# Moving all late weights behind a transpose on one DMA-issuing engine, and choosing an instruction order by its mean in noisy replays

## The chip, the cores and the metric

The kernel runs on one core of one Trainium2 chip. The metric is the device time of one execution in microseconds (us), lower is better. A run over 1.5% above the fastest of its kernel counts as "slow" and is left out. The "granted clock" is the share of full speed at which PE was allowed to run.

Engines in the listings: PE is the matmul engine (PEld its weight load), DVE the vector engine, ACT the scalar engine, POOL the GpSimd engine, SP the engine that issues nearly all DMA here (SPq in a listing is its DMA issuing).

## The reference, cut to what matters

Two layers, each a linear-attention block A and a gated block B, applied twice with the same weights to a 2048 x 512 sequence:

```python
def reference(A_x, A_wqkv, A_w_phi, A_wo, B_x, B_W_gate, B_W_up, B_W_down):
    # A: q, k, v = x @ wqkv ; phi = softmax(+-(. @ w_phi)) ; kv = sum over the sequence of phi_k * v
    #    out = (phi_q @ kv) / (phi_q @ z) @ wo
    # B: (relu(x @ W_gate) * (x @ W_up)) @ W_down
    x = A_x
    x = x + _A_ref(_layernorm(x), A_wqkv, A_w_phi, A_wo)
    x = x + _B_ref(_layernorm(x), B_W_gate, B_W_up, B_W_down)
    x = x + _A_ref(_layernorm(x), A_wqkv, A_w_phi, A_wo)
    x = x + _B_ref(_layernorm(x), B_W_gate, B_W_up, B_W_down)
    return x
```

The sum over the whole sequence (kv) closes the first phase: no output of A can be made before all 16 tiles of 128 rows have gone through k, v and the normalisation of phi_k.

## The kernel before

The program lists operations with what they read and write, and a list scheduler with a model of durations picks an order for every engine. Each engine then runs its instructions strictly in that order. In the first phase a tile `t` passes through:

1. layer norm "apply" into one of four buffers (`ytile`), on DVE for even tiles, on ACT for most odd ones;
2. a DMA transpose into `yT`, issued by SP (tiles 4 to 15; tiles 0 to 3 use PE);
3. k and v projections on PE, exponentials and copies on ACT;
4. a sum (`Zk`) and reciprocal (`rZk`) on DVE, then the product `phik` on POOL (half of it on DVE for tiles 14, 15);
5. accumulation `kvacc` on PE. After tile 15, DVE evicts the sums to `kvbd`, and the next phase begins.

SP also issues the late weights: eight pieces of `wo` (64 KB each), four of `Wg`, four of `Wu` (344 KB each), six of `Wd`. They are needed only after the first phase. Before, they were sprinkled among the transposes, each waiting for a `phik`:

```python
        def kv(t, n):
            ...
            for tt in range(t, t + n):
                self.kv_acc(tt, "A0")
                for _ in range(1 if 4 <= tt < 12 else 2):
                    if pieces:
                        pieces.pop(0)(self.r("phik", tt, 0))
        L(1); kv(0, 1); kv(1, 1); L(2); kv(2, 1); kv(3, 1)      # (one call a line in the kernel)
        self.compose_q(); kv(4, 2); L(3); kv(6, 2); kv(8, 2); kv(10, 2)
        self.q_proj(0, qr0, "A0")
        kv(12, 2); kv(14, 1); kv(15, 1)
        self.kv_fin("A0")
```

The scheduler tries 48 orders and kept the one with the shortest span in its model. In that model a weight costs SP 450 ns to issue and a transpose 1190 ns.

The softmax here doesn't subtract the row's maximum and nothing guards it: scores larger than these inputs give would overflow.

## Time and profile before

| | before |
|---|---|
| time, median of 3 | 396.07 us (395.46 to 396.57) |
| PE busy | 381.1 of 394.1 us |
| PE idle from 9 to 65 us, then up to 242 us | about 4.6 us, then none |
| tile 12's transpose: issued, landed | 36.81, 41.03 us |
| first `kvbd` eviction | 54.26 us |
| first Wg matmul (block B begins) | 74.85 us |

The first part of the profile of before gives busy time, share of the span and number of instructions:

```profile
PE 381.1 (97%) x2320; PEld 207.1 (53%) x2320; DVE 274.3 (70%) x634; ACT 215.8 (55%) x421; POOL 110.1 (28%) x160
```

Busy time by stretch of the kernel before (start:end, length, then each engine's busy us and instruction count, granted clock, DMA share, GB/s) shows where PE is not busy:

```profile
20.00:30.00 10.00, 9.89 (x69) 5.28 (x67) 10.00 (x18) 10.00 (x15) 9.28 (x11) 1.00 0.47 84
30.00:40.00 10.00, 9.08 (x67) 5.04 (x68) 9.12 (x13) 6.72 (x8) 10.00 (x6) 1.00 0.64 150
40.00:50.00 10.00, 9.58 (x71) 5.15 (x70) 7.82 (x11) 7.71 (x13) 7.79 (x5) 1.00 0.85 225
50.00:56.00 6.00, 5.54 (x57) 3.53 (x55) 4.61 (x10) 2.81 (x6) 3.82 (x3) 1.00 0.75 239
56.00:65.00 9.00, 6.84 (x53) 3.68 (x51) 7.18 (x23) 8.62 (x17) 0.00 (x0) 1.00 0.14 29
```

PE is the limit nearly everywhere; a change of order can win back little more than the few idle microseconds from 9 to 65 us (from 242 to 252 us there are 1.1 more). POOL has no idle time from 30 to 40 us. The timeline of SP in the kernel before (start, length of the issuing, what, how many) shows weights between the transposes:

```profile
31.81 2.58 SPq L536 DMA_TRANSPOSE yT<-ytile  x2
34.43 1.23 SPq L502 DMA_DIRECT2D wo_p<-in_A_wo_dram  x2
35.71 1.06 SPq L505 DMA_DIRECT2D Wg<-in_B_W_gate_dram  x2
36.81 1.22 SPq L536 DMA_TRANSPOSE yT<-ytile  x1
38.08 1.07 SPq L505 DMA_DIRECT2D Wg<-in_B_W_gate_dram  x2
39.20 1.19 SPq L536 DMA_TRANSPOSE yT<-ytile  x1
```

The transpose at 36.81 is tile 12's, the one at 39.20 tile 14's. Tile 12's input was ready at about 33.5 us. The chain that ended last, in order of time, passes through it:

```profile
36.81 4.22 DMA yT<-ytile
41.04 0.05 issue
41.08 1.05 PE ps L587 x4
42.14 0.02 issue
42.16 1.95 ACT expk L590 x2
```

It takes 4.22 us to land (median of all: 2.4), and k of tile 12 starts on its landing. POOL's timeline shows what that does to the `phik` products, idle time and releaser in brackets:

```profile
41.68 3.81 POOL L573 TENSOR_TENSOR expk<-expk,rZk 128x1024 bf16<-128x1024 bf16 x2 [0.62 <-DVE rZk L570]
47.08 6.74 POOL L573 TENSOR_TENSOR expk<-expk,rZk 128x1024 bf16<-128x1024 bf16 x4 [1.59 <-ACT expk L559]
```

### The profile page before, as it was taken

What the parts mean: (1) busy time and instruction counts of PE and PEld (TensorE: products, weight loads), DVE (VectorE), ACT (ScalarE), POOL (GpSimd) and SP (SyncE); (2) the same over time, 40 slices, a digit from 0 to 9 for tenths busy, and PEclk for the clock granted to TensorE, in tenths of its full rate; (3) what the DMA queues carried; (4) which work ended last, traced back from release to release, by engine and by line L of the source; (5) the groups of instructions that cost most, each with busy time, mean ns of one, the idle gap of its engine ahead of it and who ended that gap; (6) DMA issues with size and microseconds to landing.
All of it is one profiled execution on the core that took longest, in us unless ns stands there. A gap on an engine that the chain in (4) does not pass through costs nothing.

```text
span 394.1 us, 6313 instructions
## 1 busy us (share of the span) xinstructions
PE 381.1 (97%) x2320; PEld 207.1 (53%) x2320; DVE 274.3 (70%) x634; ACT 215.8 (55%) x421; POOL 110.1 (28%) x160
## 2 busy tenths in 40 slices
PE   5998997999999999999999999899999999999996
PEld 3455463676744444444444457467774454444442
DVE  5999778886865888886765777997875576421332
ACT  5897769953744412633354475997573562453440
POOL 5399741211000122383344543121101011100000
PEclk9999999999999999999999999999999999999999
DMA  6845942221211222311100110232323122100001
GB/s 189 217 86 147 240 146 53 55 54 28 55 28 27 42 54 54 68 27 15 27 14 2 27 28 2 41 68 54 68 55 67 27 42 67 29 27 0 28 27 53
DMA packets 61518, 23.00 MB, mean 58 GB/s; under 512 B 53456, under 2 KB 60464, under 8 KB 61488
## 3 DMA queue, kind: packets, MB, share of 16 engines
q1 hardware_dynamic: 60912, 22.08, 24.7%
q10 hardware_dynamic: 576, 0.52, 0.5%
q8 instruction: 18, 0.29, 0.3%
q14 instruction: 12, 0.10, 0.1%
HBM read 7.91 MB, written 2.10 MB: 25 GB/s over the span
## 4 chain that ended last, share of the span: by engine, by line
PE 83%; DVE 7%; issue 3%; DMA 3%; ACT 2%; POOL 2%; SPq 0%; DVEq 0%; POOLq 0%
PE ps L696 39%; PE ps L720 19%; PE ps L556 7%; PE ps L675 7%; PE ps L629 5%; PE ps L645 3%; PE ps L602 2%; DVE stats L516 2%; POOL expk L573 2%; DVE rZk L570 1%; DMA yT<-ytile 1%; DVE Zk L568 1%; DMA x_sb<-in_A_x_dram 1%; ACT numbf L649 1%; DMA oT<-osb 1%
## 5 line engine op out<-in xcount | busy, mean ns | idle before, releaser
L696 PE MATMUL ps<-yT,Wu 128*128 128x512 bf16 (+3 forms) x440 | 128.2, 336 | 0.0
L696 PE MATMUL ps<-yT,Wg 128*128 128x512 bf16 (+3 forms) x440 | 128.0, 336 | 0.0
L698 ACT ACTIVATE gate_sb<-ps 128x512 bf16<-128x512 f32 (+3 forms) x110 | 55.8, 512 | 100.8 <-PE ps L696 86.1
L720 PE MATMUL ps<-Wd,hT 128*128 128x512 bf16 (+1 forms) x352 | 107.7, 379 | 0.0
L573 POOL TENSOR_TENSOR expk<-expk,rZk 128x1024 bf16<-128x1024 bf16 (+1 forms) x32 | 59.6, 1879 | 31.6 <-DVE rZk L570 16.2
L520 POOL TENSOR_SCALAR rv<-mv 128x1 f32<-128x1 f32 (+1 forms) x55 | 13.0, 238 | 190.1 <-DVE mv L517 187.7
L696 PEld LDWEIGHTS ps<-yT,Wu 128*128 128x128 bf16 (+1 forms) x440 | 43.8, 100 | 33.4 <-ACT expk L703 0.8
L696 PEld LDWEIGHTS ps<-yT,Wg 128*128 128x128 bf16 (+1 forms) x440 | 43.5, 100 | 33.4 <-ACT gate_sb L698 0.9
L649 ACT ACTIVATE numbf<-ps 128x432 bf16<-128x432 f32 (+1 forms) x96 | 44.1, 500 | 18.1 <-PE ps L645 16.9
L720 PEld LDWEIGHTS ps<-Wd,hT 128*128 128x128 bf16 (+1 forms) x352 | 34.1, 98 | 36.8 <-DVE x_sb L722 0.9
L705 DVE TENSOR_TENSOR hT<-gate_sb,expk 128x512 bf16<-128x512 bf16 (+3 forms) x73 | 25.9, 355 | 34.2 <-ACT expk L703 33.0
L516 DVE BATCH_NORM_STATS2 stats<-x_sb 128x6 f32<-128x512 bf16 x64 | 42.7, 683 | 4.8 <-DMA x_sb<-in_A_x_dram 4.5
L568 DVE TENSOR_REDUCE Zk<-expk 128x64 f32<-128x1024 bf16 x32 | 37.9, 1202 | 6.3 <-ACT expk L559 3.1
L675 PE MATMUL ps<-wo_p,oT 128*128 128x512 bf16 x128 | 39.9, 379 | 1.6 <-DMA oT<-osb 1.6
L722 DVE TENSOR_TENSOR x_sb<-x_sb,ps 128x512 bf16<-128x512 bf16 x32 | 21.7, 685 | 27.1 <-PE ps L720 27.0
L703 ACT ACTIVATE expk<-ps 128x512 bf16<-128x512 f32 (+3 forms) x73 | 36.1, 497 | 1.1 <-PE ps L696 1.0
L645 PE MATMUL ps<-kvbd,expq 128*128 128x144 bf16 x256 | 35.1, 226 | 0.9 <-ACT numbf L649 0.6
L629 PE MATMUL ps<-yT,Wqp 128*128 128x512 bf16 x128 | 34.7, 379 | 0.9 <-ACT expq L632 0.7
L521 POOL TENSOR_TENSOR rstd<-rv,mhalf 128x1 f32<-128x1 f32 (+1 forms) x55 | 34.0, 620 | 4.1
L632 ACT ACTIVATE expq<-ps 128x1024 bf16<-128x1024 f32 (+1 forms) x40 | 32.4, 858 | 4.2 <-PE ps L629 3.8
L708 DVE TENSOR_TENSOR hT<-gate_sb,ps 128x512 bf16<-128x512 bf16 (+2 forms) x37 | 22.6, 614 | 16.8 <-PE ps L696 14.4
L559 ACT ACTIVATE expk<-ps 128x512 bf16<-128x512 f32 x44 | 23.8, 596 | 19.2 <-PE ps L556 18.9
(57 smaller groups left out, 393.3 us busy)
## 6 DMA issues: line engine op xcount, KB each, us to landing
out_dram<-x_sb SPq DMA_DIRECT2D x16, 128.0 KB, 1.7
x_sb<-in_A_x_dram SPq DMA_DIRECT2D x3, 512.0 KB, 6.1
Wg<-in_B_W_gate_dram SPq DMA_DIRECT2D x4, 344.0 KB, 4.2
Wu<-in_B_W_up_dram SPq DMA_DIRECT2D x4, 344.0 KB, 4.5
Wd<-in_B_W_down_dram SPq DMA_DIRECT2D x5, 256.0 KB, 3.3
yT<-ytile SPq DMA_TRANSPOSE x60, 2.4
hT<-in_A_wqkv_dram ACTq DMA_DIRECT2D x4, 128.0 KB, 3.0
x_sb<-in_A_x_dram SPq DMA_DIRECT2D x4, 128.0 KB, 3.7
```

The source lines that it names most:

```text
L516: op("dve", (lambda t: lambda e: e.bn_stats(k.stats6[:, t, :], k.x_sb[:, t, :]))(t), [r("x", t)], [r("st", t)], 685, f"{tag} stats {t}")
L521: op("pool", lambda e: e.tensor_tensor(k.rstd[:, t0:t1, :], k.rv1[:, t0:t1, :], k.mhalf[:, 0:n], ALU.pow), [r("rv1", t) for t in ts] + [r( ...
L568: op("dve", lambda e: e.tensor_reduce(k.Zk[:, zb, :], k.expk[:, t, :, :].rearrange("p s (h f) -> p (s h) f", f=16), AX.X, ALU.add), [r("ex ...
L573: op(eng, (lambda s0, s1: lambda e: e.tensor_tensor(k.expk[:, t, s0:s1, :].rearrange("p s (h f) -> p (s h) f", f=16), k.expk[:, t, s0:s1, ...
L629: op("pe", (lambda c, ic, bank: lambda e: e.matmul(k.pb[bank][:], k.Wqp[:, ic, c * 128:(c + 1) * 128], k.yT[:, ic, st * 512:(st + 1) * 512 ...
L645: op("pe", (lambda s, c, j, g0, bank: lambda e: e.matmul(k.pb[bank][:, j * GW:(j + 1) * GW], k.expq[:, st, c, s, tt * 128:(tt + 1) * 128], ...
L649: op("act", (lambda g0, n, bank: lambda e: e.activation(k.numbf[:, b, g0:g0 + n, :], k.pb[bank][:, 0:n * GW].rearrange("p (g m) -> p g m", ...
L675: op("pe", (lambda c, bank: lambda e: e.matmul(k.pb[bank][:], k.oT[:, ob, c, :], k.wo_p[:, c, :], start=(c == 0), stop=(c == NC - 1)))(c, ...
L696: op("pe", (lambda bank, W, ic, fc, Mf: lambda e: e.matmul(k.pb[bank][0:Mf, 0:n], W[:, ic, fc * 128:fc * 128 + Mf], k.yT[:, ic, c0:c0 + n] ...
L698: op("act", (lambda Mf, gb, gs: lambda e: e.activation(k.gate_sb[0:Mf, gs, 0:n], k.pb[gb][0:Mf, 0:n], ACT.Relu))(Mf, gb, gs), [self.RP[gb] ...
L703: op("act", (lambda Mf, ub, tu: lambda e: e.activation(k.expk[0:Mf, tu, 0, 0:n], k.pb[ub][0:Mf, 0:n], ACT.Copy))(Mf, ub, tu), [self.RP[ub] ...
L720: op("pe", (lambda fc, Kf, u, c0: lambda e: e.matmul(k.pb[bank][:], k.hT[0:Kf, u, c0:c0 + 128], k.Wd[0:Kf, fc, :], start=(fc == 0), stop=( ...
```

## The change

Its intent: SP first issues all transposes of the first phase, then all late weights, in one block. And of the 48 candidate orders, the one with the lowest mean span over six replays with noisy durations is taken, to be robust against errors of the model.

```diff
+    TRIALS = 6
...
+        rng = random.Random(1)
+        noise = [[rng.uniform(0.92, 1.08) for _ in ops] for _ in range(self.TRIALS)]
...
-                span = max(finish)
+                span = self._replay(order, noise)
...
+    def _replay(self, order, noise):
+        ...   # run the fixed order with each duration times its noise, return the mean of the spans
...
             for tt in range(t, t + n):
                 self.kv_acc(tt, "A0")
-                for _ in range(1 if 4 <= tt < 12 else 2):
-                    if pieces:
-                        pieces.pop(0)(self.r("phik", tt, 0))
...
         L(3)
+        for i, piece in enumerate(pieces):
+            piece(self.r("yT", 15 if i < 8 else 15))
         kv(6, 2)
```

Each piece now depends on the transpose of tile 15. That tile has the highest number, but the scheduler is free to issue another tile's transpose after it. The order of SP in the built kernel, by operation names:

```
before: tr 4 5 6 7 | wo0 wo1 | tr 9 11 | wo2 wo3 | tr 8 | wo4 wo5 | tr 13 15 10 | wo6 wo7 Wg0 Wg1 | tr 12 | Wg2 Wg3 | tr 14 | Wu Wd
after:  tr 4 5 6 7 9 8 11 13 10 15 12 | wo0 ... wo7 | tr 14 | Wg0 Wu0 Wg2 Wu3 Wg1 Wu2 Wg3 Wu1 | Wd
```

More of the change, by code (lines that the diff above doesn't have):

```diff
@@ L1 @@
+import random
 from contextlib import ExitStack
@@ L141, in schedule @@
                 prio = [t - o.boost for t, o in zip(self._backward(start, finish), ops)]
-        self.makespan, start, finish, order = best
+        _, start, finish, order = best
+        self.makespan = max(finish)
         for o in ops:
@@ L201, in _forward @@
         return start, finish, order
+    def _replay(self, order, noise):
+        ops = self.ops
+        total = 0.0
+        for f in noise:
+            free = {e: 0.0 for e in ENG_NAMES}
+            fin = [0.0] * len(ops)
+            q_free = 0.0
+            for i in order:
+                o = ops[i]
+                t = free[o.eng]
+                for d in o.deps:
+                    t = max(t, fin[d] + (self.SAME_LAT if ops[d].eng == o.eng else self.SYNC_LAT))
+                free[o.eng] = t + o.dur * f[i]
+                if o.is_dma:
+                    q_free = max(t + self.DMA_FIXED * 0.35, q_free) + o.dma_bytes / self.DMA_BW * (3 * f[i] - 2)
+                    fin[i] = q_free + self.DMA_FIXED * 0.65 * (5 * f[i] - 4)
+                else:
+                    fin[i] = free[o.eng]
+            total += max(fin)
+        return total / len(noise)
     def _backward(self, start, finish):
```

## The prediction

The prediction was written before any run of the changed kernel. Its "order listing" is a comparison of the two built programs, instruction by instruction on each engine.

> **What bounds the kernel now.** TensorE: the profile's first part gives PE 381.1 us of a 394.1 us span, the chain of waits 83%. Sixteen 128x512 matmuls in that chain take 3.46 us, and both kernels issue 880,896 matmul columns, so the pure stream is an estimated 372 us. Of the 22 us lost, most lie in the first 9 us and from 9 to 65 us, about 3 after the last matmul. From 65 to 242 and from 252 to 383 us PE is never idle (busy time by stretch): nothing is to be had there.
>
> **What the change does.** Same instructions, same bytes; only orders move. By the order listing POOL moves one phik, ACT and DVE agree from the first GLU stretch on, SP moves the weights. Before, eight wo pieces (0.62 us of SP each) and four Wg pieces (0.53) stand between the twelve yT transposes (1.2 to 1.3 each). Tile 12's, ready at about 33.5 us, is issued at 36.81 and lands 4.22 us later (median 2.4); its k projection starts at 41.08, at that landing. That starves ACT, then DVE (2.19 us idle before Zk 12 at 44.1), then POOL: idle 0.62 us before 41.68 and 1.59 before 47.08. Otherwise POOL runs the phik products without a gap from 25.8 to 53.8 us, 1.91 us each, and the last ends the phase (the chain shows phik, kvacc, kvbd).
>
> **What that is worth.** After: eleven transposes, all wo (5.0 us), tile 14's transpose, Wg/Wu interleaved, Wd. Tile 12 lands at about 36 us, so k of 12 and 13 starts some 3 us sooner. Tile 14's transpose stays at 39 to 40 us, no longer slowed by Wg. POOL caps the gain: the gaps are 2.2 us, plus at most 0.3 to 0.5 from its earlier second product. I expect the first kvbd at 52.0 instead of 54.26 us.
>
> Given back: all of Wg, Wu, Wd (4.2 MB) is issued from about 40.5 us; at the 240 GB/s that the slices show that takes an estimated 17.5 us, to 58, where it was over at about 56. The first oT transposes, then due at 57, meet its end. (The Trainium skill, "DMA: Bandwidth & Descriptors", Queues, rings and completion order: descriptors are consumed in ring order; tile 12's 4.22 us agrees.) I take 0.3 us off. The next stretch, to 75 us, is held by ACT (8.6 of 9, then 9.5 of 10 us busy) and only shifts. The noise-averaged choice changes no work and, where PE is saturated, nothing that counts: 0 ± 0.5 us.
>
> **Prediction: 394.0 us**, 8 in 10 between 392.4 and 395.6. Faster by over 2%: 0.02, within 2%: 0.97, slower by over 2%: 0.01.
>
> **What would show each step.** Right: the SP queue has its yT transposes back to back and the eleventh by 35 us; POOL idles under 0.6 us from 26 us to its last phik, which ends at 51 to 52; the first Wg matmul (74.85) starts near 72.9; from then on the traces run 2 us apart to the end. Wrong: POOL still idles before tiles 12 to 15; the first oT transpose takes over 3.5 us or is issued behind Wd; PE waits on Wg, Wu or Wd.
>
> **What would make it wrong.** Tile 14 behind eight wo pieces lands after 43 us and becomes the new wait; weights collide with oT transposes more than I think; the new order of q and wo matmuls between 56 and 75 us stalls ACT or DVE; or the shift is absorbed later, from 242 to 252 us or in the tail.

## The result, and the profile after

The changed kernel took 395.77 us (median of 4, 395.43 to 395.92), the kernel before 395.94 (4 runs). The ratio was 0.9994, 95% interval 0.9976 to 1.0011. A ratio is the mean time of one kernel's fast runs over that of the other's in the same rounds, so it is not quite the ratio of the medians. The prediction's 394.0 us (392.4 to 395.6) was missed. A later set of six runs (below, `after_again`) came out lower, 394.49 us and 0.9965; the change is taken to be worth about 0.8 us (the interval of the first set includes no change at all, that of the second does not): the average, weighted by runs, of 0.25 us (four runs, 395.73 against 395.98 in the mean) and 1.24 us (six, 394.70 against 395.94).

Line numbers of the changed kernel are 27 higher: L536 became L563 (transposes), L502 L529 (wo), L556 and L587 became L583 and L614 (k and v), L573 L600 (`phik`), L602 L629 (`kvacc`), L613 L640 (`kvbd`), L629 L656 (q).

SP's timeline in the changed kernel, for the same stretch:

```profile
31.61 5.95 SPq L563 DMA_TRANSPOSE yT<-ytile  x3
37.60 5.62 SPq L529 DMA_DIRECT2D wo_p<-in_A_wo_dram  x8
43.26 1.27 SPq L563 DMA_TRANSPOSE yT<-ytile  x1
44.57 0.58 SPq L532 DMA_DIRECT2D Wg<-in_B_W_gate_dram  x1
```

The first line merges three transposes over 5.95 us, gaps included: tile 10 at 31.61, then tile 15 at 35.05, then tile 12 at 36.29. Tile 12's input was ready at 33.3 us, but in SP's order it stands behind tile 15's, and tile 15's apply ran on ACT only at 34.20 to 35.02. Then come eight wo pieces, 5.62 us of SP, and only then tile 14's transpose, at 43.26 instead of 39.20 us. The chain that ended last in the changed kernel:

```profile
38.78 2.12 DVE ytile L560
40.90 0.47 DVE rZk L597
...
41.51 1.75 POOL expk L600
43.26 2.61 DMA yT<-ytile
45.87 0.05 issue
45.91 1.04 PE ps L583 x4
46.95 0.46 PE ps L629 x8
```

This has to be read with care. The chain puts a POOL instruction before the transpose, but the transpose's input, tile 14's apply, was done at 40.90. What filled the time until 43.22 is SP itself, issuing wo; issuing a DMA does not count as busy, so the chain passes it over. The timeline of SP shows it. PE's timeline in the changed kernel then has the wait:

```profile
43.51 1.02 PE L583 MATMUL ps<-Wkp,yT 128*128 128x512 bf16 x4
45.91 1.04 PE L583 MATMUL ps<-Wkp,yT 128*128 128x512 bf16 x4 [1.38 <-DMA yT<-ytile]
...
53.99 1.09 PE L629 MATMUL ps<-vsb,expk 128*128 128x129 bf16 x16
```

The first line is k of tile 15, the second k of tile 14. From 45.91 to 52.7 us PE then works without a pause through what had piled up behind tile 14, and waits once more, 0.42 us, for a q bank. The last `kvacc` (third line) start only at 53.99 us, although POOL had its last product done at 52.44. POOL's timeline after:

```profile
41.51 1.93 POOL L600 TENSOR_TENSOR expk<-expk,rZk 128x1024 bf16<-128x1024 bf16 x1 [0.76 <-ACT expk L617]
44.10 8.34 POOL L600 TENSOR_TENSOR expk<-expk,rZk 128x1024 bf16<-128x1024 bf16 x5 [0.66 <-DVE rZk L597]
```

Against the kernel before POOL ends 1.4 us earlier (52.44 against 53.82) with less idle time (0.76 and 0.66 against 0.62 and 1.59 us). But the eviction `kvbd` starts 0.3 us later, at 54.55. That 0.3 us says little by itself, because a trace as a whole can be shifted against another. Measured from an early landmark on PE (given below), `kvbd` comes after 31.57 us here and after 31.64 before. The phase is as long as it was, though POOL is done sooner. The wait had moved from POOL's side of the phase to PE's.

Busy time by stretch in the changed kernel:

```profile
30.00:40.00 10.00, 9.89 (x77) 5.75 (x77) 8.88 (x11) 8.20 (x11) 10.00 (x6) 1.00 0.44 79
40.00:50.00 10.00, 8.57 (x63) 4.72 (x63) 9.18 (x12) 6.92 (x11) 8.45 (x6) 1.00 0.62 185
50.00:56.00 6.00, 4.89 (x54) 3.51 (x54) 4.45 (x8) 2.24 (x5) 2.45 (x2) 1.00 1.03 385
56.00:65.00 9.00, 7.49 (x57) 4.15 (x56) 6.92 (x24) 8.47 (x16) 0.00 (x0) 1.00 0.37 100
```

Some matmul records are missing from this trace (2278 of 2320 are there), so small differences in PE's busy time mean little; the large ones stand. PE won 0.81 us from 30 to 40 us (9.89 against 9.08) and lost 1.01 us from 40 to 50 (8.57 against 9.58) and 0.65 us from 50 to 56 (4.89 against 5.54). The weights now move at up to 385 GB/s (239 before in the same stretch). From 56 to 65 us PE is busier than before. PE's waits there, first in the kernel before, then in the changed one:

```profile
60.17 1.16 PE L645 MATMUL ps<-kvbd,expq 128*128 128x144 bf16 x8 [0.60 <-ACT numbf L649]
62.07 0.60 PE L675 MATMUL ps<-wo_p,oT 128*128 128x512 bf16 x2 [0.74 <-DMA oT<-osb]
64.22 0.60 PE L629 MATMUL ps<-yT,Wqp 128*128 128x512 bf16 x2 [0.68 <-ACT expq L632]
```

```profile
60.45 1.16 PE L672 MATMUL ps<-kvbd,expq 128*128 128x144 bf16 x8 [0.82 <-ACT numbf L676]
62.17 0.82 PE L656 MATMUL ps<-yT,Wqp 128*128 128x512 bf16 x3 [0.55 <-ACT expq L659]
```

The new order does seven q matmuls before the first wo matmuls, so PE no longer waits for the first oT transpose: 1.37 us idle against 2.02, 0.65 us gained. That was not in the prediction's sum, and it is why the span is 0.3 us shorter though `kvbd` came 0.3 us later. The other traces confirm it: from `kvbd` to the first Wd matmul it is 30.80 to 30.83 us in the three fast traces with the PE order of before, and 30.02 to 30.03 in the seven with the new one; from that matmul to the end it is 309.1 to 309.3 us in all ten.

### The profile page after: what moved, and what is told of

Its sections match the earlier page's. It is cut to its first block, busy times and chain, and to the rows that moved or that the text cites. A ratio compares the mean times of both kernels' runs of the same rounds, so it can differ in the third digit from the quotient of the medians.

```text
span 393.8 us, 6268 instructions
## 1 busy us (share of the span) xinstructions
PE 377.8 (96%) x2278; PEld 207.2 (53%) x2320; DVE 274.9 (70%) x634; ACT 215.6 (55%) x421; POOL 109.8 (28%) x160
## 4 chain that ended last, share of the span: by engine, by line
PE 89%; ACT 4%; DVE 3%; DMA 2%; issue 1%; POOL 0%; SPq 0%; ACTq 0%; POOLq 0%
PE ps L723 38%; PE ps L747 19%; PE ps L583 10%; PE ps L702 6%; PE ps L656 6%; PE ps L672 3%; PE ps L614 3%; PE ps L629 3%; ACT expq L659 1%; DMA x_sb<-in_A_x_dram 1%; ACT numbf L676 1%; DVE ytile L560 1%; DMA yT<-ytile 1%; ACT expk L617 0%; DVE stats L543 0%
## 5 line engine op out<-in xcount | busy, mean ns | idle before, releaser
L723 PE MATMUL ps<-yT,Wu 128*128 128x512 bf16 (+3 forms) x434 | 126.0, 336 | 0.3
L723 PE MATMUL ps<-yT,Wg 128*128 128x512 bf16 (+3 forms) x433 | 125.6, 336 | 0.6 <-ACT expq L659 0.2
L747 PE MATMUL ps<-Wd,hT 128*128 128x512 bf16 (+1 forms) x341 | 104.8, 379 | 0.5
L600 POOL TENSOR_TENSOR expk<-expk,rZk 128x1024 bf16<-128x1024 bf16 (+1 forms) x32 | 59.1, 1865 | 31.0 <-DVE rZk L597 20.6
L702 PE MATMUL ps<-wo_p,oT 128*128 128x512 bf16 x124 | 38.2, 379 | 1.0 <-DMA oT<-osb 0.8
L730 ACT ACTIVATE expk<-ps 128x512 bf16<-128x512 f32 (+3 forms) x73 | 36.1, 497 | 1.1 <-PE ps L723 1.0
L656 PE MATMUL ps<-yT,Wqp 128*128 128x512 bf16 x123 | 33.1, 379 | 1.5 <-ACT expq L659 1.4
(57 smaller groups left out, 392.4 us busy)
```

Source lines behind the costliest of these rows:

```text
L600: op(eng, (lambda s0, s1: lambda e: e.tensor_tensor(k.expk[:, t, s0:s1, :].rearrange("p s (h f) -> p (s h) f", f=16), k.expk[:, t, s0:s1, ...
L656: op("pe", (lambda c, ic, bank: lambda e: e.matmul(k.pb[bank][:], k.Wqp[:, ic, c * 128:(c + 1) * 128], k.yT[:, ic, st * 512:(st + 1) * 512 ...
L702: op("pe", (lambda c, bank: lambda e: e.matmul(k.pb[bank][:], k.oT[:, ob, c, :], k.wo_p[:, c, :], start=(c == 0), stop=(c == NC - 1)))(c, ...
L723: op("pe", (lambda bank, W, ic, fc, Mf: lambda e: e.matmul(k.pb[bank][0:Mf, 0:n], W[:, ic, fc * 128:fc * 128 + Mf], k.yT[:, ic, c0:c0 + n] ...
L747: op("pe", (lambda fc, Kf, u, c0: lambda e: e.matmul(k.pb[bank][:], k.hT[0:Kf, u, c0:c0 + 128], k.Wd[0:Kf, fc, :], start=(fc == 0), stop=( ...
```

## The experiments

Theory 1: the transposes held up by weights on SP are what costs, and in the changed kernel the eight wo pieces ahead of tile 14's transpose eat the gain. Theory 2: the end of the phase is set by the order of q, k and `kvacc` on PE and ACT, whatever SP does. Theory 3, for tile 12: its late transpose does not matter, PE and ACT hold it. A rival to all: the noise-averaged choice, not the placement, decides.

Most experiments move single DMA issues after the scheduler has run, by changing their start time in its result. All other engines keep their order; the data dependencies stay, but for wo's wait on a transpose, which no data needs, in two kernels. All kernels gave correct results. Times in us; "difference" is the mean of the fast runs less the mean of the kernel before in the same rounds. The kernel before had 11 or 12 runs in each. Medians are of the fast runs (five in place_only and after_tr14_first, six in the others).

One thing can inflate the differences. Of the 34 runs of the kernel before in these sets, 11 were granted 0.996 of the clock; every fast run with the PE order of the changed kernel was granted 0.999 or 1.0. With runs under 0.999 left out on both sides the gains shrink by 0.1 to 0.4 us (after_tr14_first -1.65, tr14_first_again -1.58, after_again -0.99). Whether the order brings on the lower clock is not shown.

| kernel | median | difference | ratio, 95% interval |
|---|---|---|---|
| place_only | 395.65 | -0.65 | 0.9985 (0.9959 to 1.0010) |
| choice_only | 396.03 | +0.06 | 1.0000 (0.9979 to 1.0021) |
| after_tr14_first | 394.15 | -1.86 | 0.9954 (0.9933 to 0.9975) |
| tr14_first_again | 394.39 | -1.93 | 0.9952 (0.9931 to 0.9973) |
| before_weights_last | 394.84 | -1.22 | 0.9970 (0.9951 to 0.9990) |
| four_wo_first | 394.15 | -2.38 | 0.9941 (0.9922 to 0.9960) |
| four_wg_first | 395.07 | -1.37 | 0.9966 (0.9947 to 0.9986) |
| wo_gaps | 394.18 | -2.20 | 0.9949 (0.9932 to 0.9967) |
| before_wg_last | 396.01 | -0.19 | 0.9995 (0.9976 to 1.0013) |
| gaps_12_first | 393.98 | -2.14 | 0.9944 (0.9926 to 0.9963) |
| deps_all | 394.06 | -1.82 | 0.9952 (0.9930 to 0.9975) |
| after_again | 394.49 | -1.24 | 0.9965 (0.9943 to 0.9986) |

### The two halves of the change

```diff
 place_only, against the changed kernel:
-                span = self._replay(order, noise)
+                span = max(finish)
```

> The placement half of the change alone; the order is chosen by the shortest model span as before. Its order listing differs from the changed kernel's only in a few neighbours (two pairs on ACT and DVE, the order among Wg and Wu). Theory 1 (the placement makes the whole result, the way of choosing next to nothing): 395.8 us, within 0.3 of the changed kernel, tile 14's transpose issued near 43.3 us, PE idle about 1.4 us before k of tile 14. Rival (the noise-averaged choice cost what the placement won): about 394 us.

Measured: 394.1 to 396.3 us in five fast runs; the profiled run (granted clock 0.56) is not used. The built program differs from the changed kernel's only in a few neighbours. The time lies within the spread of the changed kernel's; the rival's 394 us was met by two runs of five, but so it was by runs of the changed kernel itself (`after_again`). What the expectation says of tile 14's transpose could not be checked.

```diff
 choice_only, against the changed kernel: the old placement put back
+                for _ in range(1 if 4 <= tt < 12 else 2):
+                    if pieces:
+                        pieces.pop(0)(self.r("phik", tt, 0))
...
-        for i, piece in enumerate(pieces):
-            piece(self.r("yT", 15 if i < 8 else 15))
```

> The other half alone: the old placement of the late weights, the order chosen by its mean time in the noisy replay. Here the choice does pick another order, in the first phase and far beyond it. Theory 1 (a choice of order is worth little where PE is saturated): between 395.0 and 397.0 us. Rival (the averaged choice gains by itself, and the placement gave it back): under 394.8 us. Rival the other way (the averaged choice loses by itself): over 397 us.

Measured: no difference. With the old placement the noisy choice picks quite another order, and its time is that of the kernel before. So the noise-averaged choice gained nothing that these runs can see, alone or with the placement; the rest of the study is about the placement and the order that the scheduler draws around it.

### One transfer moved

```diff
 after_tr14_first, after scheduling (shortened):
+            last = at["L0 tr 14"]
+            late = sorted((late weights issued before it), key=lambda o: o.start)
+            for j, o in enumerate(late):
+                o.start = last.start + 0.001 * (j + 1)
```

> The changed kernel with one transfer moved: tile 14's transpose goes ahead of the eight wo pieces on SP, all other engines and the rest of SP keep their order. Theory 1 (the eight wo issues, 5.6 us of SP, hold up tile 14's transpose, and that wait eats the gain): the transpose is issued near 41.0 instead of 43.26 us, when its input is ready, and lands near 43.4 instead of 45.87; PE's idle 1.38 us before k of tile 14 is gone, first kvbd at about 53.1 instead of 54.55, total 394.3 to 394.7 us. Rival, theory 2 (the new order of q, k and kvacc on PE and ACT at the end of the phase limits it anyway): kvbd moves by under 0.5 us, total 395.3 us or more.

Measured: 393.6 to 394.6 us in five fast runs; the profiled run was slow (clock 0.76).

> The same kernel as the one with tile 14's transpose ahead of wo, run again because its profile fell in a slow state (granted clock 0.76). Its fast runs gave 394.2 us. Theory 1: the profile shows tile 14's transpose issued near 41.0 us and landing near 43.4, no PE idle of over 0.3 us before k of tile 14, first kvbd near 53.1 us; total 394.0 to 394.6 us. Theory 2 (the gain came from elsewhere): the transpose is early but kvbd is still later than 54 us.

Measured: 394.39 us; the profile is fast. SP, PE, POOL and DVE in this kernel:

```profile
34.80 5.53 SPq L563 DMA_TRANSPOSE yT<-ytile  x3
40.38 5.15 SPq L529 DMA_DIRECT2D wo_p<-in_A_wo_dram  x8
```

```profile
43.27 1.89 PE L583 MATMUL ps<-Wkp,yT 128*128 128x512 bf16 x8
...
52.53 1.10 PE L629 MATMUL ps<-vsb,expk 128*128 128x129 bf16 x16 [0.17 <-POOL expk L600]
```

```profile
43.85 8.62 POOL L600 TENSOR_TENSOR expk<-expk,rZk 128x1024 bf16<-128x1024 bf16 x5 [1.13 <-DVE rZk L597]
```

```profile
53.09 1.02 DVE L640 TENSOR_TENSOR kvbd<-ps,mask 128x384 bf16<-128x384 f32 x2 [1.53 <-PE ps L629]
```

Tile 14's transpose (the last of the three) is issued before wo, k of tiles 15 and 14 run as one block of eight matmuls, PE's idle 1.38 us is gone, and `kvbd` starts at 53.09, as theory 1 had it, instead of 54.55 us. POOL's last product ends at 52.47, where it did in the changed kernel (52.44); PE now stands ready and waits 0.17 us for it. Theory 2 falls. One mark was missed: the transpose went at 39.08, not near 41.0, and landed at 41.53, because tile 14's apply on DVE took 0.52 us here and not 2.12 (the end of this document has more on that). This is no rival cause: in `after_again` the apply was as quick, done at 39.15, and the transpose still went only at 43.36; in `four_wo_first` the apply ended as late as 41.33, and PE did not wait.

POOL still idles 1.13 us before 43.85, for tile 12. The chain that ended last runs from k of 12, which starts at 39.06 behind other PE work, through ACT's exponentials (40.12) and DVE's sum and reciprocal to that product.

Wherever the start of a trace shifted a little, the check is the distance from one early landmark on PE (the second group of four q-composition matmuls) to `kvbd`: 31.64 us in the kernel before, 31.57 and 31.81 in two traces of the changed kernel, 30.36 here, and in the next two kernels 30.50 (four_wo_first) and 31.58 (four_wg_first).

### How much may stand ahead of tile 14

```diff
 four_wo_first: as above, but wo0 to wo3 stay ahead of tile 14's transpose
 four_wg_first: Wg0 to Wg3 go ahead of it, all of wo behind it
```

> Half the dose: four of the eight wo pieces stay ahead of tile 14's transpose, four go behind it. Theory 1a (what counts is when SP comes to issue the transpose, and its input is ready only near 40.9 us): four pieces fill SP from 37.6 to about 40.4 us and cost nothing, so the transpose is issued near 41.0 and the total is that of the kernel with none ahead, 394.0 to 394.7 us. Rival (each piece ahead costs its share, by its traffic or its issue): half of the loss, 394.8 to 395.3 us, with the transpose issued near 42.1 us or landing more than 3 us after its issue.

Measured: 394.15 us, no worse than with none ahead; the rival's half loss was not met. Tile 14's apply ended at 41.33 us in this trace and its transpose went at 41.70, landing 2.6 us later. The four pieces took SP until 41.66 (3.56 us, more than expected, since one of them took 1.56), 0.3 us past the apply. That costs nothing, because PE comes to k of 14 only behind k of 15, which starts at 44.02. The profiled run was the slowest of the six (395.0).

> Four Wg pieces (344 KB each) stand ahead of tile 14's transpose, all eight wo pieces behind it. Four Wg issues took about 2 us of SP in the kernel before, so by issue time alone the transpose still goes at its input's time, near 41.0 us. Theory 1a (issue time alone): total 394.0 to 394.7 us, landing within 3 us. Theory 1b (bytes queued ahead delay the landing too, as for tile 12's transpose in the kernel before, 4.22 us): 1.4 MB at the 320 GB/s of the changed kernel's busiest slice is an estimated 4.4 us of traffic begun near 38 us, so landing 3.5 to 5 us after issue, at 44.5 to 46, total 394.9 to 396 us.

Measured: 395.07 us. SP, the transpose's time to landing (the last line of a view of that tile) and PE:

```profile
37.91 3.88 SPq L532 DMA_DIRECT2D Wg<-in_B_W_gate_dram  x4
41.84 1.21 SPq L563 DMA_TRANSPOSE yT<-ytile  x1
```

```profile
DMA to landing us min/median/max: 4.3/4.3/4.3
```

```profile
46.16 1.04 PE L583 MATMUL ps<-Wkp,yT 128*128 128x512 bf16 x4 [1.31 <-DMA yT<-ytile]
```

Theory 1b held: it lands 4.3 us after issue. But theory 1a's premise fell too: four Wg issues took 3.88 us of SP, not 2, and tile 14's input, ready at 39.49, waited 2.35 us. Three of the four took 0.43 to 0.58 us; one, Wg2, took 2.31, and why is open (in `before_weights_last` four Wg in a row took 0.42 to 0.59 each). So the late landing fits the bytes ahead, while the late issue hangs on one slow piece, and the experiment does not say what either alone would cost. PE is idle 1.31 us again, and the total is about 1 us above the kernel with four wo pieces ahead (395.00 against 393.99 in the mean, same rounds).

### wo early, in SP's gaps; tile 12 ahead of tile 15

```diff
 wo_gaps: wo0-2 behind tr 7, wo3-5 behind tr 8, wo6-7 behind tr 10 (places where SP stood idle), their wait for tile 15 dropped
 gaps_12_first: the same, and tr 12 ahead of tr 15
```

> The changed kernel with the eight wo pieces put where SP stood idle in its trace (three near 22.0 us, three near 26.9, two near 33.1), without their wait for tile 15's transpose, and tile 14's transpose right behind tile 12's. Every other engine keeps its order. Theory 1: early wo pieces cost nothing as long as they sit in gaps, so as with tile 14 first, 394.0 to 394.7 us, and the big weights are issued some 2.5 us earlier than there was need for. Rival (late is better for its own sake, traffic during the transposes slows them): transposes from 24 to 38 us land over 3 us after issue and the total is 395 us or more.

Measured: 394.18 us. Theory 1 held: wo pieces between transposes do no harm as long as they sit where SP waits. "All late" is not needed as such. One mark of the rival did appear, tile 11's transpose landing 3.96 us and tile 13's 3.12 us after issue; but in the changed kernel, without any wo there, they took 3.58 and 2.95.

> The kernel with wo in SP's gaps, with one more move on SP: tile 12's transpose goes ahead of tile 15's, which has to wait for ACT until 35 us. So tile 12's lands near 36 us, as the prediction had assumed. Theory 3 (k of 12 is held by then by PE's own queue and by ACT emptying the banks, not by its transpose): k of 12 and 13 starts within 0.4 us of where it does without this move, total within 0.4 us of that kernel, 393.9 to 394.5 us. Rival (the late tile 12 cost what the prediction said): k of 12 about 1 us or more sooner, total under 393.7 us.

Measured: 393.98 us. Tile 12's transpose is issued at 33.60 and lands 2.5 us later, at 36.1, as the prediction had assumed; k of tile 13 and k of tile 12 start at 37.68 and 38.72 us, against 37.37 and 38.40 in the trace of wo_gaps: not sooner. So an earlier tile 12 gains nothing in this order: theory 3 held as far as the transpose goes. In the changed kernel too, k of tile 12 starts (39.31 us) right behind other PE work, with no wait shown before it. That PE's own queue and ACT hold it is the rest of the theory, and was not tested by itself.

### The kernel before, with only SP changed

```diff
 before_weights_last: all late weights behind tr 14 on SP, everything else in the order of before
 before_wg_last: only Wg0 to Wg3 moved behind tr 14
```

> The kernel before with only its SP order changed: all late weights behind the last of the twelve transposes, every other engine in the order of before. Theory 1 (what holds the phase in the kernel before is tile 12's transpose behind wo and Wg; taking exactly that away gives about what was predicted): tile 12's transpose is issued near 33.6 instead of 36.81 us and lands near 36, POOL's idle 0.62 and 1.59 us shrink to under 0.8 in sum, first kvbd at 52.0 to 52.8 instead of 54.26, total 394.0 to 394.8 us. Rival, theory 2 (another engine's order, not SP, sets the end of the phase): kvbd later than 53.6 us, total 395.4 us or more.

Measured: 394.84 us. Tile 12's transpose goes at 33.51 and lands 2.5 us later; POOL is idle 0.98 us (expected: under 0.8); `kvbd` starts at 52.91, 0.1 us later than expected. The direction is theory 1's, the size just short of it. The landmark distance is 30.44 us, as in the changed kernel with tile 14 first. That one is a further 0.6 us or so faster in total; the rest is the stretch after `kvbd`, 30.83 us to the first Wd matmul here against 30.03 there.

> The kernel before with only its four Wg pieces moved behind tile 14's transpose; the eight wo pieces stay between the transposes as they were, every other engine in the order of before. Theory 1 (in the kernel before it is the Wg pieces that hold tile 12's and 14's transposes, by their bytes more than by their issue; wo pieces do no harm there): tile 12's transpose is issued near 35.7 us, lands under 3 us later at about 38.3, which is before PE comes to its k (39.7 us with all weights moved), so the total is that with all late weights moved, 394.5 to 395.2 us. Rival (the two wo pieces before tile 12's transpose count as much): 395.4 to 396.2 us.

Measured: 396.01 us; theory 1 in this form fell. Tile 12's transpose went at 35.98 and landed 2.5 us later, so Wg's hold on it was gone, and the trace has `kvbd` 0.5 us nearer to the landmark (31.11 us). But an earlier wait, overlooked in the prediction, stayed. PE's timeline for k of tile 8 here, and in the kernel with all weights moved:

```profile
31.03 1.04 PE L587 MATMUL ps<-Wkp,yT 128*128 128x512 bf16 x4 [0.84 <-DMA yT<-ytile]
```

```profile
29.92 1.04 PE L587 MATMUL ps<-Wkp,yT 128*128 128x512 bf16 x4 [0.18 <-DMA yT<-ytile]
```

Two wo pieces stand directly ahead of tile 8's transpose in the order of before, where SP was not idle: 0.84 us of PE there, 0.88 in the kernel before, 0.18 with all moved. Moving wo as well shortens the landmark distance by another 0.67 us (31.11 to 30.44), as much as this wait shrank (0.84 to 0.18). So in the kernel before wo and Wg both count. The measured time of -0.19 us is less than the trace's 0.5; the interval holds both.

### The dependency as it was perhaps meant, and the changed kernel again

```diff
 deps_all (in late_weights, [rd] also became list(rd)):
-            piece(self.r("yT", 15 if i < 8 else 15))
+            piece([self.r("yT", t) for t in range(12, 16)])
```

> The changed program with its late weights made to depend on the transposes of tiles 12, 13, 14 and 15, not of 15 alone, and the order left to the scheduler, with the noise-averaged choice. On SP all twelve transposes then stand before the first wo piece, but the scheduler also picks other orders on every engine, over the whole kernel. If SP's order is what counts: 394.0 to 395.2 us. If the orders that come along matter as much: anything from 393 to 397 us, which would say that half a per cent either way can come from such a re-draw alone.

Measured: 393.8 to 394.5 us in five runs and 396.3 in the sixth, the profiled one. All twelve transposes stand ahead of the weights, and the time is that of the other kernels with tile 14 ahead. But the scheduler drew another order on every engine, so this says that this small remedy works here, not that it works for this reason alone; its trace, of the slowest run, has PE busy only 7.21 of 10 us from 20 to 30 us.

> The changed kernel itself once more, in five rounds, so that the one-move experiments can be compared with it at the same number of runs. If the first result holds (ratio 0.9994 to the kernel before): 395.4 to 396.2 us, tile 14's transpose issued over 2 us after its input is ready or right behind the last wo piece, PE idle over 1 us before k of tile 14. If the first result was a fluctuation and the change does gain what was predicted: under 394.6 us.

Measured: 393.88, 393.88, 394.08, 394.89, 395.65 and 395.83 us. By the median (394.49) the "fluctuation" of the first result was partly one; by the mean (394.70) neither expectation was met. The profiled run was one of the two longest of the six (395.65) and shows the known picture: tile 14's transpose at 43.36, PE idle 1.62 us before its k. No trace fell on a run at 394 us, so why one kernel gives both 393.9 and 395.8 is open. (place_only, with the same order in this phase, gives both as well: 394.1 to 396.3.)

## Why the prediction was wrong, point by point

- **What bounds the kernel: right.** PE is never idle in the long stretches of before, and all gains and losses that the traces show lie before the first Wd matmul at about 85 us, nearly all before 65.
- **Tile 14's transpose "stays at 39 to 40 us": wrong, and this is the step that failed.** It was issued at 43.26. The block of wo was sized about right (5.0 predicted, 5.62 measured), but its start was not: it began at 37.60, not near 35, because tile 15's transpose stood ahead of it and waited until 35.02 for ACT, whose order the change had also moved (before, ACT was done with tile 15's apply by 30.0). The prediction took the old trace's times for inputs and did not walk SP's new queue with the new order of ACT. It had named this as what would make it wrong ("tile 14 behind eight wo pieces lands after 43 us and becomes the new wait"); it landed at 45.87. PE stood idle 1.38 us for it, and the first Wg matmul started at 75.22, not near 72.9. Moving that one transpose forward took the gain from some 0.8 us to 1.9 us (1.86 and 1.93). By the totals alone this is not firm: the intervals of `after_again` and `tr14_first_again` overlap, and only ten runs against eleven (-0.84 and -1.89 in the mean) stand apart; the traces carry it. That 1.9 is so near the 2.07 us forecast is luck in part: the landmark distance to `kvbd` shrank by 1.28 us, not by the 2.26 forecast, and 0.8 us came from the stretch after it, for which nothing was forecast.
- **Tile 12 "lands at about 36 us", k of 12 "some 3 us sooner": wrong in both; the transpose was harmless, k was not.** The transpose was issued at 36.29, and k started 1.8 us sooner (39.31 against 41.08). Forcing the landing to 36.1 us changed the time by nothing that could be seen, so the prediction was wrong to hang k on the landing: in the new order k starts right behind other PE work. With tile 14 out of the way, that k is what POOL still waits for (1.13 us), and `kvbd` comes at 53.09, not 52.0.
- **POOL caps the gain: right only once tile 14 is out of the way.** POOL's last product ended at 52.44 (51 to 52 predicted) with 1.4 us of idle time left (under 0.6 predicted), and PE, not POOL, held `kvbd`, at 54.55 against 52.0 predicted. With tile 14 first, PE waits for POOL again.
- **0.3 us given back to late weight traffic: not seen.** The estimate used 240 GB/s; the stretch from 50 to 56 us of the changed kernel shows 385. The last Wd piece, issued at 52.25, took 7.3 us and landed at about 59.5, and the first oT transpose, issued at 59.84, took 2.5. In the kernel with tile 14 first one of the first oT transposes took 3.3 us, and PE did not wait for it.
- **"0 ± 0.5 us" for the noise-averaged choice: held,** alone (+0.06) and with the placement.
- **"The next stretch only shifts": wrong by 0.65 us, to the good.** PE's idle time from 56 to 65 us fell from 2.02 to 1.37 us, and `kvbd` to the first Wd matmul is 0.8 us shorter in every trace of the new order.
- **The range.** The first result lay 0.17 us above it; the ten runs of the changed kernel average 395.1 us, inside, but the gain of about 0.8 us is still under half of the forecast.

The best versions run here beat both kernels by small amounts: four wo pieces ahead 394.15 us, wo in the gaps 394.18, tile 12 ahead of 15 as well 393.98. Their intervals overlap; they are not told apart.

## What to carry to other kernels

When transfers move on an engine that issues DMA in order, walk the whole new queue: for every transfer write down when its input is ready under the new order of the engine that makes it, and add up the issue times of all that stand before it. "Behind the last one" must name the last one in issue order, not the one with the highest number. Cheap transfers can go early into gaps where the queue waits anyway; large ones belong behind everything urgent, because they can delay the landing of what stands behind them (here 4.3 us behind four Wg pieces, 2.6 behind wo).

## What the Trainium skill lacked or had wrong

- "DMA: Bandwidth & Descriptors", Issuing engines are not separate DMA queues, says of a sequencer's time to initiate a DMA that it "is usually small relative to the DMA itself". Here it was not: a 64 KB wo piece took SP 0.70 us to issue on average (5.62 us for eight) against 2.5 us to landing, and a transpose 1.2 to 1.3 against 2.4; eight such issues were the wait that cost the gain.
- The same page gives no issue time by shape. Here it did not follow the bytes: a 64 KB wo piece (16 partitions) took 0.59 to 0.68 us in the changed kernel (one of the eight 1.08), and a 344 KB Wg piece 0.43 to 0.58 us. Single pieces took far longer than their like (Wg2 2.31 us in four_wg_first); no run here shows why.
- The same page, Queues, rings and completion order, says that each DMA engine takes descriptors in ring order. What it lacks is a size for this: a transpose behind four Wg pieces landed after 4.3 us, against 2.6 us behind eight or four wo pieces. That fits the page but does not prove it: in before_weights_last tile 14's transpose took 4.0 us with no weight ahead of it.
- "SBUF — State Buffer", SBUF: two separate sides, describes an exclusive lock between DVE and POOL. The changed kernel's trace agrees: tile 14's apply on DVE took 2.12 us where tile 12's took 0.37, ending 0.15 us after a POOL product that ran from 38.83 to 40.75 us; in four_wo_first it took 2.05 and again ended 0.15 us after the product. What the page lacks is how far chance decides it: with the same order on both engines the same apply took 0.40 to 0.84 us in five other traces. Since SP was held by wo until 43.22, it cost nothing here.
- "Perfetto Trace Analysis", DMA Instruction — HWDGE (DVE, Sync), says that the issuing engine is free for its next instruction only after a DMA's descriptors have been generated, and that the data movement is not in that time. The runs agree. What the page lacks is the consequence for a chain of waits: in the changed kernel the chain named a POOL product (41.51 us) before a transpose that was in truth held 2.3 us, from 40.90 to 43.22, by SP's own earlier issues. The DMA queue's timeline is needed beside it.
